# The down projection of tiles 2 to 4 as seven half-size products, with the sums on GpSimd

## The chip, the cores and the metric

The kernel runs on one core of a Trainium2 chip. The metric is the device time of one execution in microseconds (us). The engines are TensorE (PE, with its weight loads PEld), VectorE (DVE), ScalarE (ACT), GpSimd (POOL) and SyncE (SP), which here only issues transfers. A kernel of this size can be told from another by about 0.2%.

## The reference

A layer of 2048 tokens with 512 features: normalisation, 32 heads of sliding-window attention (16 features a head, window 256) with an output projection, and beside it a gated feed-forward network of 1792 hidden features whose result gates the attention's. All data are float32.

```python
xn = _layernorm(x, axis=-1)
qkv = (xn @ wqkv).reshape(B, S, 3, H, Dh).transpose(2, 0, 3, 1, 4)
scores = jnp.einsum("bhqd,bhkd->bhqk", q, k) * (Dh ** -0.5)
mask = (idx[:, None] - idx[None, :] >= 0) & (idx[:, None] - idx[None, :] < 256)
o = softmax(where(mask, scores, -1e9)) @ v
s = o @ wo
h = silu(xn @ w1) * (xn @ w3)
out = h @ w2
return x + s * silu(out)
```

## The kernel before

**Precision.** Each float32 operand is cut into two float16 halves, the value rounded (ACT casts) and the remainder (POOL or DVE subtracts). A product is then three matmuls: high x high, high x low, low x high. A cut tile is 128 x 1024 float16, high half first.

**Tiles.** The tokens go in four tiles of 512 (`NT`), counted 0 to 3 in the code. The hidden features go in 14 blocks of 128 (`FB`), in `GROUPS` whose down projections are summed in one bank each. For each tile and block, `gate_up` makes gate and up (24 matmuls of 512 columns), ACT takes a tanh (L867), DVE multiplies twice (L871, L876), ACT casts the hidden block (L880) and POOL subtracts its remainder (L300, by the helper `halves`, in two pieces of 256 columns). For each group, `down` runs over the four blocks of 128 tokens: three matmuls of 512 columns for each hidden block into one bank (L901). The first group's bank is copied by ACT (L914), the others are added by DVE (L917) to a sum in SBUF. `total` then gates: tanh of the sum (L937), a product on DVE (L938), the output projection of the attention (L943), a product with its bank (L947), the residual (POOL by `halves`, for the last tile DVE at L949), and the store. The last block of 128 tokens of all is done by `total_by_columns` in two halves of 256 columns (L965 to L976).

**Weights.** In tile 0 the weights are measured, scaled and cut (`measure`, `measure_down`; ACT at L303 and L304, POOL at L300), and the cut weights are stored to DRAM (`dW1`, `dW2`). Tiles 1 to 3 load them again (`load`).

**Attention** runs in units of four heads beside that: scores and their maxima (L588, L600), scores, mask, exponential (L662, L669, L672) and values (L690). `normalise` sends the denominators through DRAM and multiplies on POOL (`on`, by `rb`) some 8 steps later, and ACT casts the product (L740).

**Order.** PE takes its instructions in the order of the code (`ORDERED`). `feed_forward` lists the dense pieces, `spread` mixes them among the attention's batches, and a group's `down` comes after the next block's `gate_up`. For DVE, ACT, POOL and SP a scheduler sets the order beforehand; each engine then works through its own queue strictly in that order. Work for later is put off by `later(n, f)`, n steps on. All temporary tiles lie in `SLOTS` equal slots of SBUF: `take` hands out the one that was given back longest ago, and its new user waits for the last reader of the old tile. PSUM has two banks for the dense work, used in turn (`bank`).

## Time and profile before

| | before |
|---|---|
| median of 3 runs | 840.06 us (839.98 to 840.22) |
| span of the profiled execution | 835.6 us |
| start of tile 1's gate and up, about | 221 us |
| end of the last attention values | 800.8 us |
| first matmul of the last outputs (L943) | 821.5 us |
| start of the last addition | 832.6 us |

The span is the time from the first to the last instruction of the one execution that the profiler took. Matmuls are pipelined: a matmul of 512 columns is shown with 0.38 us and starts 0.216 us after the one before it.

### The profile page before, as it was taken

How to read it: one execution, taken by the hardware profiler on the slowest of the kernel's cores; microseconds unless marked ns; L12 is line 12 of the kernel's file. 1: busy time of each engine (PE TensorE's matmuls, PEld its weight loads, DVE VectorE, ACT ScalarE, POOL GpSimd, SP SyncE). 2: the span in 40 equal slices, each digit the busy share in tenths (PEclk: the TensorE clock that was granted, in tenths of full speed). 3: DMA queues.
4: the chain of work that ended last, by engine and by line, in shares of the span. 5: the costliest groups of instructions: out<-in, count | busy, mean ns of one | idle time of the engine just before them, and what ended most of it. 6: DMA issues, size and time to landing. Idle time of an engine off the chain costs nothing.

```text
span 835.6 us, 22584 instructions
## 1 busy us (share of the span) xinstructions
PE 809.6 (97%) x8750; PEld 381.5 (46%) x8750; DVE 614.4 (74%) x2034; ACT 408.2 (49%) x598; POOL 196.7 (24%) x325
## 2 busy tenths in 40 slices
PE   9999898899999999999999999999999999999998
PEld 4434344434444444444445444444444444444444
DVE  8788767966797767798778876687777777676435
ACT  6799776373436444344433444443444443443521
POOL 2236264051313203111110211121111104031211
PEclk9999999999999999999999999999999999999999
DMA  9977556146633453453442535533443443434101
GB/s 281 260 232 237 165 181 184 47 152 199 189 96 95 110 140 108 138 155 110 130 121 72 140 94 154 142 111 102 119 143 88 112 117 107 116 96 125 55 21 52
DMA packets 95323, 110.62 MB, mean 132 GB/s; under 512 B 17200, under 2 KB 60528, under 8 KB 95216
## 3 DMA queue, kind: packets, MB, share of 16 engines
q1 hardware_dynamic: 94928, 108.67, 44.9%
q8 instruction: 68, 1.11, 0.6%
q10 hardware_dynamic: 288, 0.52, 0.2%
q14 instruction: 39, 0.32, 0.1%
HBM read 76.28 MB, written 28.57 MB: 125 GB/s over the span
## 4 chain that ended last, share of the span: by engine, by line
PE 68%; DVE 9%; issue 7%; DMA 6%; ACT 5%; POOL 3%; SPq 2%; POOLq 0%; ACTq 0%; DVEq 0%
PE m L856 24%; PE m L901 13%; PE po L690 8%; PE m L534 6%; PE s L662 5%; PE m L943 4%; PE m L504 3%; POOL slot L300 3%; DVE junk L600 2%; PE s L588 2%; DMA slot<-in_B_w_dram 2%; DMA qa<-dQ 1%; DVE s L669 1%; PE po L588 1%; ACT slot L303 1%
## 5 line engine op out<-in xcount | busy, mean ns | idle before, releaser
L300 POOL TENSOR_TENSOR slot<-slot,slot 128x256 f16<-128x256 f32 (+1 forms) x228 | 148.3, 677 | 575.7 <-ACT slot L880 464.5
L856 PE MATMUL m<-XH,slot 128*128 128x512 f16 x896 | 267.3, 380 | 4.3 <-DVE slot L547 2.5
L672 ACT ACTIVATE pt<-s,es 128x1024 f32<-128x1024 f32 x152 | 167.7, 1113 | 180.5 <-DVE s L669 177.3
L856 PEld LDWEIGHTS <-slot 128*128 128x128 f16 x1344 | 124.8, 98 | 159.9 <-issue 17.7
L856 PE MATMUL m<-XL,slot 128*128 128x512 f16 x448 | 169.8, 379 | 0.0
L901 PE MATMUL m<-slot,slot 128*128 128x512 f16 x672 | 158.1, 383 | 2.2 <-DVE slot L917 1.0
L669 DVE TENSOR_TENSOR s<-s,MK 128x256 f32<-128x256 f32 (+2 forms) x280 | 118.6, 435 | 49.2 <-PE s L662 48.2
L600 DVE CUSTOM_DVE_ANT_0 junk<-s,MW 128x320 bf16<-128x320 f32 x276 | 134.3, 486 | 24.7 <-PE s L588 15.7
L901 PEld LDWEIGHTS <-slot 128*128 128x128 f16 x672 | 62.5, 98 | 82.2 <-issue 12.3
L600 DVE CUSTOM_DVE_ANT_0 junk<-po,MW 128x320 bf16<-128x320 f32 x172 | 83.7, 487 | 5.6 <-DVE al L272 0.4
L690 PE MATMUL po<-pt,V 64*32 64x320 f32 (+4 forms) x2880 | 77.7, 343 | 0.5 <-DVE pp L277 0.5
L880 ACT CAST slot<-slot 128x512 f16<-128x512 f32 x56 | 34.5, 616 | 67.4 <-DVE slot L876 67.1
L690 PEld LDWEIGHTS po<-pt,V 64*32 64x32 f32 x2880 | 51.9, 106 | 24.1 <-PE s L588 4.7
L662 PE MATMUL s<-qa,KA 50*64 50x320 f16 (+3 forms) x1472 | 58.0, 259 | 1.4 <-DVE M L600 0.6
L871 DVE SCALAR_TENSOR_TENSOR slot<-slot,m 128x512 f32<-128x512 f32 x56 | 38.3, 684 | 28.0 <-ACT slot L867 27.0
L662 PEld LDWEIGHTS <-KA 50*64 50x64 f16 x1472 | 30.2, 105 | 55.7 <-issue 36.1
L867 ACT ACTIVATE slot<-m,sgs 128x512 f32<-128x512 f32 x56 | 38.4, 685 | 27.8 <-PE m L856 27.6
L588 PE MATMUL s<-KA,qa 48*64 48x320 f16 (+2 forms) x648 | 45.3, 294 | 6.7 <-DVE M L600 4.0
L917 DVE SCALAR_TENSOR_TENSOR slot<-m,dsc,slot 128x512 f32<-128x512 f32 x48 | 35.9, 747 | 15.9 <-PE m L901 15.6
L876 DVE SCALAR_TENSOR_TENSOR slot<-m,slot 128x512 f32<-128x512 f32 x56 | 38.5, 688 | 12.3 <-PE m L856 11.4
L534 PE MATMUL m<-XH,whi 128*128 128x512 f16 x120 | 44.7, 381 | 1.4 <-DVE slot L876 0.9
L534 PE MATMUL m<-XL,whi 128*128 128x512 f16 x120 | 44.5, 379 | 0.0
(152 smaller groups left out, 870.7 us busy)
## 6 DMA issues: line engine op xcount, KB each, us to landing
slot<-dW SPq DMA_DIRECT2D x126, 256.0 KB
slot<-in_B_w_dram SPq DMA_DIRECT2D x42, 256.0 KB
dW<-slot SPq DMA_DIRECT2D x42, 256.0 KB
slot<-in_A_x_dram SPq DMA_DIRECT2D x30, 256.0 KB
KA<-dK SPq DMA_DIRECT2D x24, 288.0 KB
qa<-dQ SPq DMA_DIRECT2D x32, 192.0 KB
dQ<-slot SPq DMA_DIRECT2D x16, 256.0 KB
dK<-slot SPq DMA_DIRECT2D x16, 256.0 KB
```

What stands on the lines that cost most here:

```text
L300: op(out[:, c], a[:, c], b[:, c])
L534: nc.tensor.matmul(cell["pp"], a[:, k, c, :], b[:, c, :], start=(c, i) == parts[0][0], stop=(c, i) == parts[-1][-1])
L588: nc.tensor.matmul(s[64 * c:64 * c + 64, r, :n], qa[rows, 2 * p + a, ii * P + 64 * c:ii * P + 64 * c + 64], ka[rows, 2 * p + a, e - n:e], ...
L600: nc.vector.tensor_tensor_reduce(out=junk[:, :n], in0=s[:, r, :n], in1=mask, scale=1.0, scalar=NEG, op0=ALU.add, op1=ALU.max, accum_out=M[ ...
L662: nc.tensor.matmul(s[64 * h:64 * h + 64, r, o:o + 64 * n], ka[rows, 2 * p + a, 64 * (m + 4):64 * (m + 5)], qa[rows, 2 * p + a, 64 * (m + k ...
L669: nc.vector.tensor_add(v, v, MK[:, kind, of:of + n, :].unsqueeze(1).to_broadcast([P, 2 * len(which), n, 64]))
L672: nc.scalar.activation(pt, s, AF.Exp, scale=es)
L690: nc.tensor.matmul(cell["po"][32 * i:32 * i + 32, h, 64 * (m + k):64 * (m + k + n)], V[64 * h:64 * h + 64, (4 * t + m // 2) % VB, hd * VW: ...
L856: nc.tensor.matmul(cell[k], w[:, (a * NC + c) * P:(a * NC + c + 1) * P], b[:, c, :], start=c == 0 and i == 0, stop=c == NC - 1 and i == 2)
L867: nc.scalar.activation(sg, cell[0], AF.Tanh, scale=sg_scale[:, f:f + 1])
L876: nc.vector.scalar_tensor_tensor(sg, cell[1], 0.5 * HS / (WS * XS)**2, sg, op0=ALU.mult, op1=ALU.mult)
L901: nc.tensor.matmul(ps, hh[:, a * TW + b * P:a * TW + (b + 1) * P], w[:, c * D:(c + 1) * D], start=f == f0 and i == 0, stop=f == f1 - 1 and ...
```

## The change

The down projection of tiles 1 to 3 is a product of a token x hidden and a hidden x output matrix. Two neighbouring hidden blocks are taken as the two halves of the inner dimension, the tile's 512 tokens as two halves of 256, the 512 outputs as two halves of 256. The 2 x 2 x 2 block product, eight half-size products, is made as seven (Strassen's scheme, in Winograd's order with 15 sums). `PRODUCTS` names them: each takes one sum of token halves on the left (`lefts`, made for every pair of blocks on POOL and cast by ACT) and one sum of weight halves on the right (`sums`, made in tile 0 on POOL, cast by ACT, stored to the new DRAM tensor `dWT`). A product has, for each of two blocks of 128 tokens and each pair of hidden blocks, three matmuls of 256 columns. Its bank goes to a sum of its own (`SUMS`), copied by ACT for the first group and added by DVE for the others. After the last group `combine` makes seven additions of 128 x 512 (on POOL, for the last tile on DVE).

The right-hand slices are loaded product by product, two products ahead (`rights`, `AHEAD`); tiles 1 to 3 no longer load `dW2` whole. Three groups of 4, 6 and 4 blocks take the place of four. Outputs are multiplied, added and stored in halves of 256 columns. The outputs of tiles 1 and 2 come two units of attention later than before. There are 46 slots, and the room for them is taken from a scratch area of the compiler's (`dynamic_dma_scratch_size`).

```diff
-SLOTS = 39
+SLOTS = 46
-GROUPS = ((0, 4), (4, 8), (8, 11), (11, 14))
+GROUPS = ((0, 4), (4, 10), (10, 14))
+PRODUCTS = ("12 21", "22 -4", "11 11", "s3 t3", "s1 t1", "s2 t2", "s4 22")
+LEFT = {"11": (0, 0), "12": (1, 0), "22": (1, 1), "s1": (2, 0), "s2": (2, 1), "s3": (3, 0), "s4": (3, 1)}
+RIGHT = {"11": (0, 0), "21": (1, 0), "22": (1, 1), "t1": (2, 0), "t2": (2, 1), "t3": (3, 0), "-4": (3, 1)}
+AHEAD = 2
...
+    dWT = dram.tile([FB, P, 2 * D], F16, name="dWT")
...
     def load(t, f):
         if t:
-            WF[t, f] = a, b = [take(F16) for _ in range(2)], take(F16)
+            WF[t, f] = a, _ = [take(F16) for _ in range(2)], None
             for k in range(2):
                 nc.sync.dma_start(a[k], dW1[f, k])
-            nc.sync.dma_start(b, dW2[f])
             return
...
+            def sums(f):
+                e, o = whole.pop(f), whole.pop(f + 1)
+                a, b = take(F32), take(F32)
+                left, right = slice(0, 256), slice(256, 512)
+                nc.gpsimd.tensor_sub(a[:, left], e[:, right], e[:, left])
+                nc.gpsimd.tensor_sub(a[:, right], o[:, right], a[:, left])
+                nc.gpsimd.tensor_sub(b[:, left], o[:, right], e[:, right])
+                nc.gpsimd.tensor_sub(b[:, right], o[:, left], a[:, right])
+                give(e, o, after=5)
+                for i, raw in enumerate((a, b)):
+                    made = take(F16)
+                    nc.scalar.copy(made[:, 0:D], raw)
+                    halves(nc.gpsimd.tensor_sub, made[:, D:], raw, made[:, 0:D])
+                    nc.sync.dma_start(dWT[f + i], made)
+                    give(raw, made, after=6)
             for i, f in enumerate(range(f0, f1)):
                 later(1 + 2 * i, lambda f=f: cut(f))
+                if f % 2:
+                    later(2 * n + 2 + 4 * i, lambda f=f: sums(f - 1))
...
+    def lefts(t, f):
+        e, o = WHOLE.pop((t, f)), WHOLE.pop((t, f + 1))
+        a, b = take(F32), take(F32)
+        one, two = slice(0, 256), slice(256, 512)
+        def cast(i, raw, c):
+            made = LH[t, f][i]
+            nc.scalar.copy(made[:, c], raw[:, c])
+        def rest(i, raw, c):
+            made = LH[t, f][i]
+            nc.gpsimd.tensor_sub(made[:, D + c.start:D + c.stop], raw[:, c], made[:, c])
+        LH[t, f] = [take(F16), HH.pop((t, f + 1)), take(F16), take(F16)]
+        cast(1, o, slice(0, 512))
+        cast(0, e, one)
+        nc.gpsimd.tensor_add(a[:, one], e[:, two], o[:, two])
+        nc.gpsimd.tensor_sub(b[:, one], e[:, one], e[:, two])
+        nc.gpsimd.tensor_sub(a[:, two], a[:, one], e[:, one])
+        nc.gpsimd.tensor_sub(b[:, two], o[:, one], a[:, two])
+        cast(3, b, slice(0, 512))
+        cast(2, a, slice(0, 512))
+        for i, raw, c in ((1, o, one), (1, o, two), (0, e, one), (3, b, one), (2, a, one), (2, a, two), (3, b, two)):
+            rest(i, raw, c)
+        give(e, o, a, b, after=5)
...
-                later(1, rest)
+                if t == 0:
+                    later(1, rest)
+                elif f % 2:
+                    later(1, lambda: lefts(t, f - 1))
...
+    def rights(t, k, p):
+        i, which = RIGHT[PRODUCTS[p].split()[1]]
+        c = slice(256 * which, 256 * which + 256)
+        f0, f1 = GROUPS[k]
+        made = []
+        for j in range(f0, f1, 4):
+            slot = take(F16)
+            made.append(slot)
+            for n, f in enumerate(range(j, min(j + 4, f1), 2)):
+                src = (dW2[f], dW2[f + 1], dWT[f], dWT[f + 1])[i]
+                nc.sync.dma_start(slot[:, n * D:(n + 1) * D].rearrange("p (a c) -> p a c", a=2),
+                                  src.rearrange("p (a c) -> p a c", a=2)[:, :, c])
+        RIGHTS[t, k, p] = made
+
+    def product(t, k, p):
+        f0, f1 = GROUPS[k]
+        i, which = LEFT[PRODUCTS[p].split()[0]]
+        def part():
+            ps = bank([P, 2, 256])
+            right = RIGHTS.pop((t, k, p))
+            fs = range(f0, f1, 2)
+            for blk in range(2):
+                q = 256 * which + 128 * blk
+                for f in fs:
+                    n = (f - f0) // 2
+                    l, r = LH[t, f][i], right[n // 2][:, (n % 2) * D:(n % 2 + 1) * D]
+                    for x, (a, c) in enumerate(((0, 0), (0, 1), (1, 0))):
+                        nc.tensor.matmul(ps[:, blk, :], l[:, a * D + q:a * D + q + 128], r[:, 256 * c:256 * c + 256],
+                                         start=f == f0 and x == 0, stop=f == f1 - 2 and x == 2)
+            give(*right)
...
+            if k == 0:
+                SUMS[t, p] = take(F32)
+                with urgent():
+                    nc.scalar.activation(SUMS[t, p], flat, AF.Copy, scale=down_scale[:, 0:1])
+            else:
+                with urgent():
+                    nc.vector.scalar_tensor_tensor(SUMS[t, p], flat, down_scale[:, k:k + 1], SUMS[t, p],
+                                                   op0=ALU.mult, op1=ALU.add)
+            if (k, p) == (len(GROUPS) - 1, len(PRODUCTS) - 1):
+                combine(t)
+        return [(3 * (f1 - f0) // 2, part)]
+
+    def combine(t):
+        p2, p4, p1, p7, p5, p6, p3 = (SUMS.pop((t, p)) for p in range(7))
+        def add(a, b):
+            if t == NT - 1:
+                nc.vector.tensor_add(a, a, b)
+            else:
+                halves(nc.gpsimd.tensor_add, a, a, b)
+        add(p2, p1)
+        add(p6, p1)
+        add(p3, p5)
+        add(p3, p6)
+        add(p7, p6)
+        add(p4, p7)
+        add(p5, p7)
...
             if half:
-                with urgent():
-                    nc.vector.scalar_tensor_tensor(y, ps, sc["y"], y, op0=ALU.mult, op1=ALU.mult)
...
+                for i, c in enumerate((slice(0, 256), slice(256, 512))):
+                    with urgent():
+                        nc.vector.scalar_tensor_tensor(y[i], ps[:, c], sc["y"], y[i], op0=ALU.mult, op1=ALU.mult)
+                    (nc.vector if t == NT - 1 else nc.gpsimd).tensor_add(y[i], y[i], XR[t, b][:, c])
+                    nc.sync.dma_start(out[r, c], y[i])
...
+                for _ in range(3 if len(late) == len(PRODUCTS) else 2):
+                    if late:
+                        pieces += products(*late.pop(0))
...
-        if 2 <= n % 8 < 6 and t:
-            beside[n] += [(0, lambda t=t, b=n % 8 - 2: residual(t - 1, b))] + total(t - 1, n % 8 - 2)
+        b = n % 8 - (2 if t == 1 else 4)
+        if 0 <= b < 4 and t:
+            beside[n] += [(0, lambda t=t, b=b: residual(t - 1, b))] + total(t - 1, b)
```

In the changed kernel the lines are L681 for the exponential, L884 and L888 for the casts and remainders of `lefts`, L892 to L895 for its sums, L854 to L857 for `sums`, L1015 for the products' matmuls, L1025 and L1028 for the sums of their banks, L1041 for the combination on DVE, L1077 for the gate's product, L1107 and L1128 for the outputs.

## The prediction

> **What bounds the kernel now.** I read the cores' line first (one core, its clock), then busy time by stretch, then the groups of instructions, then the waits, and last the timeline of two places: the first use of the down weights, near 77 us, and the end. The cores' line and the page's first part:

> ```profile
> core 0: 835.6 us, clock 0.998
> PE 809.6 (97%) x8750; PEld 381.5 (46%) x8750; DVE 614.4 (74%) x2034; ACT 408.2 (49%) x598; POOL 196.7 (24%) x325
> ```

> Busy time by stretch (stretch, its length, then PE, PEld, DVE, ACT and POOL, PE clock, DMA share, GB/s):

> ```profile
> 60.00:100.00 40.00, 35.76 (x316) 16.17 (x315) 32.88 (x132) 34.58 (x67) 20.56 (x32) 0.96 0.70 228
> 100.00:200.00 100.00, 90.99 (x1044) 43.79 (x1042) 75.00 (x296) 59.40 (x99) 38.67 (x60) 1.00 0.44 134
> 300.00:400.00 100.00, 98.25 (x1158) 46.15 (x1157) 82.15 (x260) 42.70 (x53) 18.86 (x28) 1.00 0.46 129
> 500.00:600.00 100.00, 100.00 (x1111) 46.51 (x1109) 72.43 (x230) 44.20 (x54) 18.92 (x29) 1.00 0.46 130
> ```

> The granted clock is full, so an average is not hiding a throttle. From 200 us on PE never rests and no other engine passes 82%: there a shorter matmul stream shortens the kernel. Up to 200 us PE is 89 to 91% busy, and between 60 and 100 us ACT is at 86% with DVE at 82%: there PE waits for others, and work added to ACT or POOL can cost time.

> **What the change does to PE.** Each of the tiles 2 to 4 spends 14 blocks x 4 token blocks x 3 = 168 matmuls of 512 columns on the down projection, 504 together. They become 7 products x 7 pairs of blocks x 2 x 3 = 294 a tile, 882 together, of 256 columns. The before kernel already runs 256-column matmuls with fresh weights each time, in its last block (timeline, PE and its weight loads):

> ```profile
> 821.47 7.93 PE L943 MATMUL m<-slot,slot 128*128 128x512 f16 x36
> 829.03 2.72 PEld L972 LDWEIGHTS <-slot 128*128 128x128 f16 x24
> 829.24 2.78 PE L972 MATMUL m<-slot,slot 128*128 128x256 f16 x24
> L901 PE MATMUL m<-slot,slot 128*128 128x512 f16 x672 | 158.1, 383 | 2.2 <-DVE slot L917 1.0
> ```

> The durations overlap, so I take the distance: (7.93 - 0.38) / 35 = 0.2157 us for 512 columns, and, with 0.27 for one, (2.78 - 0.27) / 23 = 0.109 us for 256. The weight load in between (2.72 / 24 is one every 0.11 us) stays covered. So 504 x 0.2157 - 882 x 0.109 = 108.7 - 96.1 = **12.6 us less**. Seven products instead of eight would give 13.6; half-size matmuls give 1 us of it back. If a weight load were laid bare each time the distance would be about 0.2 and the change would lose 70 us; 24 in a row at 0.109 exclude that.

> Fewer, longer dense pieces also mean fewer changes between them and attention: in PE's order 156 places after, 167 before. A change costs about 0.09: in the rows of 77 us below, the sixth matmul of a run of six starts at 77.28 + 5 x 0.216 = 78.36, and the next one 0.31 after it, not 0.216. 11 x 0.09 = **1.0 us less**.

> **What it adds.** POOL's order has 292 element-wise instructions before and 523 after, ACT's has 65 more, and SP issues 955 transfers for 821. The prices:

> ```profile
> L300 POOL TENSOR_TENSOR slot<-slot,slot 128x256 f16<-128x256 f32 (+1 forms) x228 | 148.3, 677 | 575.7 <-ACT slot L880 464.5
> L880 ACT CAST slot<-slot 128x512 f16<-128x512 f32 x56 | 34.5, 616 | 67.4 <-DVE slot L876 67.1
> L917 DVE SCALAR_TENSOR_TENSOR slot<-m,dsc,slot 128x512 f32<-128x512 f32 x48 | 35.9, 747 | 15.9 <-PE m L901 15.6
> ```

> POOL grows by 231 x 0.68 = 157 us, to 354 us or 43%; ACT by about 65 x 0.62 = 40, to 54%. Neither becomes the bound by its total. What counts is who waits in their queues.

> *The first tile.* Its matmuls are unchanged, but the weight sums (`sums`) go into POOL's queue among the cuts that PE needs. POOL before, where the down weights of the first four blocks are cut (slots 36, 37, 38 and 9 hold blocks 0 to 3; the other rows are other tiles):

> ```order
> L300 TENSOR_TENSOR slot20_1153<-slot36_732,slot20_1153 128x256 x2
> L300 TENSOR_TENSOR slot0_1165<-slot35_729,slot0_1165 128x256 x2
> L300 TENSOR_TENSOR slot21_1186<-slot37_734,slot21_1186 128x256 x2
> L300 TENSOR_TENSOR slot27_1243<-slot38_736,slot27_1243 128x256 x2
> L300 TENSOR_TENSOR slot26_1256<-slot30_1182,slot26_1256 128x256 x2
> L300 TENSOR_TENSOR slot23_1269<-slot9_824,slot23_1269 128x256 x2
> ```

> and POOL after, from just behind the cut of block 0 (blocks 1, 2, 3 are slots 37, 38, 1; one more sum stands ahead of it):

> ```order
> L855 TENSOR_TENSOR slot7_1421<-slot37_735,slot7_1421 128x256
> L856 TENSOR_TENSOR slot31_1422<-slot37_735,slot36_733 128x256
> L857 TENSOR_TENSOR slot31_1422<-slot37_735,slot7_1421 128x256
> L309 TENSOR_TENSOR slot28_1187<-slot37_735,slot28_1187 128x256 x2
> L309 TENSOR_TENSOR slot18_1244<-slot38_737,slot18_1244 128x256 x2
> L309 TENSOR_TENSOR slot19_1257<-slot15_1183,slot19_1257 128x256 x2
> L854 TENSOR_TENSOR slot15_1585<-slot38_737 128x256
> L856 TENSOR_TENSOR slot9_1586<-slot1_825,slot38_737 128x256
> L855 TENSOR_TENSOR slot15_1585<-slot1_825,slot15_1585 128x256
> L857 TENSOR_TENSOR slot9_1586<-slot1_825,slot15_1585 128x256
> L309 TENSOR_TENSOR slot20_1270<-slot1_825,slot20_1270 128x256 x2
> ```

> Eight sums now stand ahead of the cut of block 3. The timeline there, PE and POOL of before:

> ```profile
> 77.28 1.46 PE L901 MATMUL m<-slot,slot 128*128 128x512 f16 x6
> 78.67 0.42 PE L662 MATMUL s<-qa,KA 50*64 50x320 f16 x10
> 79.30 5.51 PE L901 MATMUL m<-slot,slot 128*128 128x512 f16 x24
> 91.71 0.25 PE L588 MATMUL s<-KA,qa 48*64 48x128 f16 x4 [2.92 <-DVE M L600]
> 74.31 3.82 POOL L300 TENSOR_TENSOR slot<-slot,slot 128x256 f16<-128x256 f32 x6 [0.44 <-ACT slot L304]
> 78.67 1.30 POOL L300 TENSOR_TENSOR slot<-slot,slot 128x256 f16<-128x256 f32 x2 [0.54 <-ACT slot L304]
> ```

> The cut of block 3 ends at 78.67 + 1.30 = 79.97 and PE comes to it at 79.30 + 3 x 0.216 = 79.95: nothing to spare, and POOL nearly without a pause before. Eight sums at 0.64 (six in 3.82) are 5.1 us, less the half microsecond POOL stood idle: PE stands about 4.5 us. At 91.71 it waited 2.92 us for DVE's maxima, and DVE can work its backlog off in the new hole, so some returns. Bounds 0 and 4.5; I take **+2.5**.

> *The chain for each pair of blocks, tiles 2 to 4.* `lefts` adds on POOL what ACT casts next. ACT before, at a comparable place (L672 is the exponential, L880 the cast):

> ```order
> L700 COPY os_4986<-po_4937 128x512
> L880 CAST slot6_5004<-slot11_4907 128x512
> L672 ACTIVATE pt_5025<-s_5015,es1_409 128x1024
> L867 ACTIVATE slot35_5049<-m0_5036,sgs_153 128x512
> L937 ACTIVATE slot19_5258<-slot1_1418 128x512
> L672 ACTIVATE pt_5070<-s_5059,es1_409 128x1024
> ```

> and after (L681 is the exponential, L884 the casts, of which the second and third read POOL's sums):

> ```order
> L924 ACTIVATE slot31_5501<-m1_5409,sgs_154 128x512
> L1067 ACTIVATE slot39_5742<-slot33_1455 128x512
> L681 ACTIVATE pt_5515<-s_5505,es1_410 128x1024
> L884 CAST slot34_5545<-slot31_5501 128x512
> L884 CAST slot19_5553<-slot8_5550 128x512
> L884 CAST slot1_5554<-slot42_5551 128x512
> L681 ACTIVATE pt_5588<-s_5577,es1_410 128x1024
> ```

> Two casts that wait for POOL now stand ahead of an exponential. POOL needs two additions for the first and two instructions more for the second, 1.4 and 2.7 us, against 0.62 for the cast in between: ACT stands some 1.4 us a pair, 21 pairs, 30 us. The waits of before price such a stand:

> ```profile
> ACT pt L672 <- DVE s L669: 177.3, 111, 5.3
> ACT slot L740 <- POOL on L300: 24.8, 11, 4.3
> PE s L588 <- ACT pt L672: 1.9, 3, 0.7
> POOL on L300 <- DMA rb<-de: 33.4, 6, 11.6
> ```

> (who waits, total us, times, longest). ACT already stood 24.8 us for POOL, and PE's wait for the exponential came to 1.9: ACT usually stands idle until DVE hands it the scores. By that share 30 us cost 2.3; the bounds are 0 and 5, the last if the casts themselves hurt as well. I take **+2.0**.

> *Banks and transfers.* A four-block product fills its bank in 12 x 0.109 = 1.31 us, so the bank after next must be empty by then. At the end a bank's last column passes at 826.65 (24 matmuls of L943), and DVE is through with it at 827.61:

> ```profile
> 826.86 0.75 DVE L947 SCALAR_TENSOR_TENSOR slot<-m,us,slot 128x512 f32<-128x512 f32 x1 [1.11 <-PE m L943]
> ```

> 0.96 us, so a queue of over 0.35 on DVE costs PE time. Only some 18 places in PE's order have no attention in between. With the right-hand slices, now fetched two products ahead, **+1.0**, between 0 and 3.

> *The end.* The last gate and up block is followed by seven products with no attention, then by the outputs. Before:

> ```profile
> 813.07 8.56 PE L901 MATMUL m<-slot,slot 128*128 128x512 f16 x36
> 813.27 0.69 DVE L876 SCALAR_TENSOR_TENSOR slot<-m,slot 128x512 f32<-128x512 f32 x1 [1.18 <-PE m L856]
> 823.66 0.69 DVE L966 SCALAR_TENSOR_TENSOR slot<-slot,slot 128x512 f32<-128x512 f32 x1 [0.69 <-ACT slot L965]
> 824.27 0.75 DVE L947 SCALAR_TENSOR_TENSOR slot<-m,us,slot 128x512 f32<-128x512 f32 x1
> 825.05 0.69 DVE L949 TENSOR_TENSOR slot<-slot,slot 128x512 f32<-128x512 f32 x1
> 830.84 0.48 DVE L974 SCALAR_TENSOR_TENSOR slot<-m,us,slot 128x256 f32<-128x256 f32 x1
> 831.35 0.42 DVE L975 TENSOR_TENSOR slot<-slot,slot 128x256 f32<-128x256 f32 x1
> 832.58 0.42 DVE L975 TENSOR_TENSOR slot<-slot,slot 128x256 f32<-128x256 f32 x1
> ```

> The 36 matmuls take 821.47 - 813.07 = 8.40 us, 0.63 over their 7.77: the wait for the last cast. After, the first product needs the last pair's sums: 0.89 until DVE is done, then three instructions of POOL (2.1) and hand-overs, 3.1 us, while PE has five matmuls (0.55) to do: it stands 2.5, that is 1.9 more. Then DVE, with L1028 the banks' sums, L1041 the combination, L1107 the outputs:

> ```order
> L1028 SCALAR_TENSOR_TENSOR slot0_12302<-m1_13573,dsc_156,slot0_12302 128x512
> L1041 TENSOR_TENSOR slot17_12066<-slot17_12066,slot8_12219 128x512
> L1041 TENSOR_TENSOR slot0_12302<-slot0_12302,slot43_12125 128x512
> L1041 TENSOR_TENSOR slot4_11830<-slot4_11830,slot17_12066 128x512
> L1041 TENSOR_TENSOR slot0_12302<-slot0_12302,slot8_12219 128x512
> L1107 SCALAR_TENSOR_TENSOR slot10_13601<-m0_13600,us_4361,slot10_13601 128x256
> ```

> where before the last sum (L917) one gate product and then the outputs came:

> ```order
> L917 SCALAR_TENSOR_TENSOR slot29_11383<-m0_12604,dsc_155,slot29_11383 128x512
> L966 SCALAR_TENSOR_TENSOR slot8_12680<-slot8_12680,slot29_11383 128x512
> L947 SCALAR_TENSOR_TENSOR slot15_12622<-m1_12621,us_4227,slot15_12622 128x512
> L949 TENSOR_TENSOR slot15_12622<-slot15_12622,slot28_12485 128x512
> L947 SCALAR_TENSOR_TENSOR slot32_12643<-m0_12642,us_4227,slot32_12643 128x512
> ```

> From the last product's end DVE has 25 instructions: that sum, 5 of the combination, 3 gate products, 8 outputs and 8 additions of 256 columns. Independent neighbours follow at 0.61 (823.66 to 824.27), dependent ones at 0.78 and 0.51 (824.27 to 825.05, 830.84 to 831.35). With independent spacing (0.41 and 0.35 for the short ones, their durations less the same 0.07) that is 0.4 + 9 x 0.61 + 8 x 0.41 + 8 x 0.35 = 12 us, with a few dependences 12.5; with dependent spacing throughout 14.6. Then as before 2.6 from the last addition's start (833.0) to the end. So 15.1 to 17.2, against 835.6 - 821.47 = 14.1. Most neighbours are independent: +1.4. The end costs **+3.3**, between 2.9 and 5.

> **The sum.** 835.6 - 12.6 - 1.0 + 2.5 + 2.0 + 1.0 + 3.3 = 830.8 for the profiled execution. The median of the runs (840.06) lies 4.4 above that span, which the change does not touch: **835.2 us**.

> **Rivals.** *GpSimd as the gate (slower).* POOL's queue now holds, one behind the other, the normalising products that wait for a chain of transfers (six waits, 33.4 us, up to 11.6) and the sums that ACT and PE need. While POOL stands for `rb`, ACT stands at the next cast and the exponential behind it is late. Before, nothing urgent stood behind such a wait. If four of the six come back at 5.6 us each and half of each reaches PE (11 us), I get 846. It decides from 4.9 us of stalls beyond those charged. For it: ACT at 86% and POOL without pause near 77 us. Against it: the scheduler places those products late, and 10 of 16 did not wait.

> [...]

> [...]

> [...]

> *Everything hides (faster).* First tile, exponentials and banks cost nothing and the end its lower bound: -12.6 - 1.0 + 2.9, 829.4. *The terms cancel.* Stalls near their upper bounds: no change.

> That fewer columns are not streamed is excluded by the order itself.

> **How the numbers follow.** Under 0.2% (1.7 us) a measurement of this kernel does not tell from none, so the borders are 838.4 and 841.7. Forecast 0.43 (its own range 830 to 838), everything hides 0.10, cancel 0.12, GpSimd as the gate 0.30, ports 0.05. Faster 0.53, same 0.12, slower 0.35. The range of 8 in 10 reaches from just under the fast rival to a little over the gate's 846: 829 to 848.

> **What would show it.** Products at 0.109 us and PE at 98% from 200 us on: the main term. A stand of PE near 80 us at block 3's cut: the first tile. Waits of PE for the exponential of no more than 5 us: the chain. More than 15 us from the last product to the end: the end's term. I am wrong if PE shows new idle time between 200 and 800 us released by ACT or POOL, or if the time from the start of tile 2 to the last attention does not shrink by about 10 us.

## The result: 886 us, slower by 46

The changed kernel takes 885.97 us (median of 4 runs, 884.5 to 886.86) against 840.02 for the kernel before on the same chip: a ratio of 1.056, with an interval of 1.054 to 1.057. The forecast was 835.2, its range ended at 848.

The profiled execution spans 885.1 us where it was 835.6. The cores' line and the page's first part, of the changed kernel:

```profile
core 0: 885.1 us, clock 0.974
PE 819.5 (93%) x9124; PEld 426.0 (48%) x9124; DVE 627.1 (71%) x2050; ACT 438.2 (50%) x663; POOL 352.4 (40%) x556
```

GpSimd's total came out as forecast (354), and no engine is full over the whole span. But TensorE fell from 97 to 93% busy, and its mean granted clock from 0.998 to 0.974. By stretch (columns as in the prediction):

```profile
60.00:100.00 40.00, 33.70 (x294) 14.77 (x283) 34.38 (x121) 33.67 (x64) 31.59 (x48) 0.91 0.69 225
100.00:200.00 100.00, 82.62 (x902) 38.98 (x901) 68.08 (x257) 57.96 (x100) 50.01 (x76) 0.95 0.46 145
300.00:400.00 100.00, 93.68 (x1091) 47.51 (x1090) 71.89 (x233) 48.76 (x65) 38.02 (x58) 0.98 0.45 124
500.00:600.00 100.00, 98.18 (x1144) 51.60 (x1141) 72.12 (x229) 49.33 (x66) 43.12 (x65) 1.00 0.43 115
```

Only the third tile (500 to 600 us) looks as foreseen. The products and the waits that the prediction named, from the groups and from the waits of the changed kernel (who waits, for whom, total us, times, longest):

```profile
L1015 PE MATMUL m<-slot,slot 128*128 128x256 f16 x882 | 108.4, 278 | 6.3 <-ACT slot L884 4.7
```

```profile
PE s L597 <- ACT pt L681: 14.7, 12, 4.0
PE s L671 <- ACT pt L681: 6.9, 5, 2.4
ACT slot L884 <- POOL slot L894: 27.0, 21, 4.6
ACT slot L884 <- POOL slot L895: 9.2, 14, 0.7
POOL on L309 <- DMA rb<-de: 59.5, 10, 13.3
DVE dr L736 <- DMA dr<-dd: 18.2, 9, 4.2
```

TensorE waits 21.6 us for exponentials (2.4 before), ScalarE 36 us for GpSimd's sums (30 forecast). The median distance between two products' matmuls is 0.109 us, as forecast; all their distances together make 113.6 us, not 96.1.

**Where the time goes**, by the distances from each matmul's start to the next (sums over a run's trace, us):

| matmuls | before | grouping alone | no sums | changed |
|---|---|---|---|---|
| gate and up | 304.9 | 314.8 | 316.5 | 318.0 |
| down, products included | 155.6 | 152.8 | 148.7 | 162.0 |
| scores (two lines) | 96.6 | 97.6 | 102.5 | 119.1 |
| all the rest | 274.7 | 272.7 | 277.3 | 281.9 |
| start of the last matmul | 831.8 | 837.8 | 844.9 | 881.0 |

("Grouping alone" is the run x1 and "no sums" the run z3, both told below.) A stand is time in which an engine waits. The changed kernel's time went to almost every line, most of all to the scores.

**Three places of the changed kernel**, read across engines. First, the use of block 3's cut; PE, ACT and POOL in turn:

```profile
82.08 1.04 PE L963 MATMUL m<-slot,slot 128*128 128x512 f16 x4
84.66 1.67 PE L963 MATMUL m<-slot,slot 128*128 128x512 f16 x7 [1.55 <-POOL slot L309]
80.23 1.14 ACT L861 CAST slot<-slot 128x512 f16<-128x512 f32 x2
83.39 0.62 ACT L861 CAST slot<-slot 128x512 f16<-128x512 f32 x1 [2.02 <-POOL slot L857]
81.81 0.72 POOL L855 TENSOR_TENSOR slot<-slot,slot 128x256 f32<-128x256 f32 x1
82.61 0.74 POOL L857 TENSOR_TENSOR slot<-slot,slot 128x256 f32<-128x256 f32 x1
83.32 13.34 POOL L309 TENSOR_TENSOR slot<-slot,slot 128x256 f16<-128x256 f32 x20
```

GpSimd makes the sums (L855, L857) while TensorE comes to the cut behind them and stands 1.55 us. That was forecast. Not forecast is the last row: 13 us of cuts and remainders queue up behind them without a pause. Second, the start of the fourth tile, POOL, ACT and PE:

```profile
728.17 8.26 POOL L309 TENSOR_TENSOR slot<-slot,slot 128x256 f32<-128x256 f32 x12
738.44 0.72 POOL L894 TENSOR_TENSOR slot<-slot,slot 128x256 f32<-128x256 f32 x1
739.19 0.62 ACT L884 CAST slot<-slot 128x512 f16<-128x512 f32 x1 [4.56 <-POOL slot L894]
741.02 1.11 ACT L681 ACTIVATE pt<-s,es 128x1024 f32<-128x1024 f32 x1
742.18 0.48 PE L597 MATMUL s<-KA,qa 48*64 48x320 f16 x4 [3.96 <-ACT pt L681]
```

The combination of the third tile (12 of its 14 halves, 8.26 us) delays the sums of a pair, the cast stands 4.56 us for them, the exponential behind the cast is late, TensorE stands 3.96. Third, the end, DVE and then PE:

```profile
855.87 0.35 DVE L736 RECIPROCAL dr<-dr 128x32 f32<-128x32 f32 x1 [4.20 <-DMA dr<-dd]
856.40 0.68 DVE L933 SCALAR_TENSOR_TENSOR slot<-m,slot 128x512 f32<-128x512 f32 x1
857.79 0.61 PE L1015 MATMUL m<-slot,slot 128*128 128x256 f16 x2 [4.65 <-ACT slot L884]
859.37 10.89 PE L1015 MATMUL m<-slot,slot 128*128 128x256 f16 x79 [0.97 <-POOL slot L888]
```

VectorE stood 4.20 us for a transfer of the normalisation, with the last gate product (L933) queued behind it; so the last pair's operands came late. SyncE's queue shows how that transfer (L732) was issued:

```profile
850.28 0.52 SPq L719 DMA_DIRECT2D dd<-os  x1
850.90 1.24 SPq L996 DMA_DIRECT2D slot<-dWT  x2
852.24 1.21 SPq L996 DMA_DIRECT2D slot<-dW  x2
853.55 0.54 SPq L732 DMA_DIRECT2D dr<-dd  x1
```

Between the store of the denominators and their load stand four loads of half rows for the products (L996), 2.45 us of issuing. In the run x3 below the store goes out at 829.50 and the load at 831.22, and the reciprocal does not wait.

### The profile page after: what moved, and what is told of

Its sections match the earlier page's. It is cut to its first block, busy times and chain, and to the rows that moved or that the text cites. A ratio compares the mean times of both kernels' runs of the same rounds, so it can differ in the third digit from the quotient of the medians.

```text
span 885.1 us, 23936 instructions
## 1 busy us (share of the span) xinstructions
PE 819.5 (93%) x9124; PEld 426.0 (48%) x9124; DVE 627.1 (71%) x2050; ACT 438.2 (50%) x663; POOL 352.4 (40%) x556
## 4 chain that ended last, share of the span: by engine, by line
PE 49%; POOL 12%; DVE 10%; ACT 9%; DMA 8%; issue 8%; SPq 3%; ACTq 0%; POOLq 0%; DVEq 0%
PE m L913 20%; POOL slot L309 7%; PE po L699 6%; PE m L1015 6%; PE m L543 5%; ACT pt L681 3%; PE s L671 3%; PE m L1102 2%; DVE junk L609 2%; PE m L513 2%; DMA dr<-dd 2%; DVE s L678 2%; PE s L597 2%; SPq L996 1%; ACT slot L312 1%
## 5 line engine op out<-in xcount | busy, mean ns | idle before, releaser
L913 PE MATMUL m<-XH,slot 128*128 128x512 f16 x896 | 271.1, 385 | 9.4 <-DVE slot L556 2.6
L681 ACT ACTIVATE pt<-s,es 128x1024 f32<-128x1024 f32 x152 | 167.6, 1112 | 161.4 <-DVE s L678 160.3
L913 PEld LDWEIGHTS <-slot 128*128 128x128 f16 x1344 | 125.3, 98 | 166.1 <-issue 27.3
L309 POOL TENSOR_TENSOR slot<-slot,slot 128x256 f16<-128x256 f32 (+1 forms) x176 | 114.9, 687 | 139.4 <-ACT slot L939 45.4
L1015 PE MATMUL m<-slot,slot 128*128 128x256 f16 x882 | 108.4, 278 | 6.3 <-ACT slot L884 4.7
L1015 PEld LDWEIGHTS <-slot 128*128 128x128 f16 x882 | 86.2, 100 | 27.9 <-ACT slot L884 4.9
L884 ACT CAST slot<-slot 128x256 f16<-128x256 f32 (+1 forms) x84 | 47.4, 564 | 98.5 <-DVE slot L933 61.9
L888 POOL TENSOR_TENSOR slot<-slot,slot 128x256 f16<-128x256 f32 x147 | 95.5, 673 | 1.6 <-ACT slot L884 1.5
L892 POOL TENSOR_TENSOR slot<-slot,slot 128x256 f32<-128x256 f32 x21 | 15.3, 727 | 135.0 <-DVE slot L933 135.0
L928 DVE SCALAR_TENSOR_TENSOR slot<-slot,m 128x512 f32<-128x512 f32 x56 | 38.3, 684 | 42.4 <-ACT slot L924 40.3
L893 POOL TENSOR_TENSOR slot<-slot 128x256 f32<-128x256 f32 x21 | 15.2, 725 | 131.0 <-DVE slot L933 77.5
L671 PE MATMUL s<-qa,KA 50*64 50x320 f16 (+3 forms) x1472 | 59.0, 261 | 7.4 <-ACT pt L681 6.9
L597 PE MATMUL s<-KA,qa 48*64 48x320 f16 (+2 forms) x648 | 47.4, 299 | 18.9 <-ACT pt L681 14.7
L671 PEld LDWEIGHTS <-KA 50*64 50x64 f16 x1472 | 30.9, 106 | 58.0 <-issue 43.7
L597 PEld LDWEIGHTS <-qa 48*64 48x64 f16 x1024 | 31.6, 108 | 46.2 <-issue 31.4
L924 ACT ACTIVATE slot<-m,sgs 128x512 f32<-128x512 f32 x56 | 38.3, 684 | 28.1 <-PE m L913 27.9
```

Source lines behind the costliest of these rows:

```text
L309: op(out[:, c], a[:, c], b[:, c])
L597: nc.tensor.matmul(s[64 * c:64 * c + 64, r, :n], qa[rows, 2 * p + a, ii * P + 64 * c:ii * P + 64 * c + 64], ka[rows, 2 * p + a, e - n:e], ...
L671: nc.tensor.matmul(s[64 * h:64 * h + 64, r, o:o + 64 * n], ka[rows, 2 * p + a, 64 * (m + 4):64 * (m + 5)], qa[rows, 2 * p + a, 64 * (m + k ...
L681: nc.scalar.activation(pt, s, AF.Exp, scale=es)
L884: nc.scalar.copy(made[:, c], raw[:, c])
L888: nc.gpsimd.tensor_sub(made[:, D + c.start:D + c.stop], raw[:, c], made[:, c])
```

## Experiments

Each run stands beside runs of the kernel before on its own chip; the last columns compare with those. "All" is the changed kernel. Where two runs' intervals overlap, the difference between them is not clear of noise.

| run | us | before | ratio, interval | difference |
|---|---|---|---|---|
| all | 886.0 | 840.0 | 1.056 [1.054, 1.057] | +45.9 |
| x1 grouping alone | 843.5 | 839.8 | 1.005 [1.003, 1.007] | +3.8 |
| x2 all, no weight sums | 871.6 | 839.8 | 1.040 [1.035, 1.044] | +31.8 |
| x3 all, no left sums | 863.7 | 839.8 | 1.028 [1.026, 1.030] | +24.0 |
| x4 all, last tile plain | 871.4 | 839.8 | 1.037 [1.035, 1.040] | +31.6 |
| z3 all, no sums | 851.9 | 839.0 | 1.016 [1.013, 1.019] | +12.9 |
| y1 combination on VectorE | 881.8 | 838.2 | 1.051 [1.049, 1.054] | +43.6 |
| y2 left casts later | 885.5 | 838.2 | 1.055 [1.052, 1.058] | +47.2 |
| y3 weight casts later | 878.2 | 838.2 | 1.049 [1.044, 1.054] | +40.0 |
| y4 y1 to y3 together | 877.0 | 838.2 | 1.047 [1.044, 1.050] | +38.8 |
| u1 left casts on GpSimd | 891.1 | 840.5 | 1.059 [1.054, 1.063] | +50.6 |
| u2 weight casts on GpSimd | 893.8 | 840.5 | 1.064 [1.061, 1.067] | +53.4 |
| z1 products spread | 886.0 | 839.0 | 1.056 [1.053, 1.059] | +47.0 |
| w1 normalisation later | 889.5 | 839.0 | 1.061 [1.058, 1.065] | +50.4 |
| z2 matmuls at the end | 885.5 | 839.0 | 1.056 [1.052, 1.060] | +46.5 |
| v1 no sums, no reload | 847.0 | 837.7 | 1.010 [1.008, 1.012] | +9.3 |
| v2 no sums, no combination | 848.5 | 837.7 | 1.013 [1.010, 1.016] | +10.8 |
| v3 no sums, no normalising | 851.3 | 837.7 | 1.016 [1.014, 1.017] | +13.6 |
| v4 before, no normalising | 850.3 | 837.7 | 1.012 [1.009, 1.016] | +12.6 |

How late four of the 152 exponentials start, and the end, against the profiled execution before (there at 241, 336, 682, 786 and 835.6 us):

| run | 241 | 336 | 682 | 786 | end |
|---|---|---|---|---|---|
| x1 | +4.6 | +5.3 | +6.4 | +6.3 | +6.1 |
| all | +20.1 | +29.8 | +34.2 | +41.8 | +49.4 |
| x2 | +3.1 | +12.5 | +18.5 | +26.0 | +33.4 |
| x3 | +18.4 | +24.4 | +23.6 | +25.1 | +26.9 |
| x4 | +21.7 | +24.5 | +35.4 | +35.7 | +34.8 |
| z3 | +5.1 | +11.6 | +11.2 | +11.8 | +13.3 |
| v1 | +2.0 | +7.4 | +5.3 | +5.6 | +7.3 |
| v4 | +11.9 | +14.3 | +13.5 | +13.2 | +13.5 |

The profiled span before, 835.6 us, lies 4.4 under the median of its runs, and the others mostly 1 to 3 under theirs; so the last column differs from the differences above by up to 3.5 us.

### What the parts cost

x1, in the kernel before (with it, as in the changed kernel, the downs in pieces of two blocks and the smaller scratch area):

```
-SLOTS = 39
+SLOTS = 46
-GROUPS = ((0, 4), (4, 8), (8, 11), (11, 14))
+GROUPS = ((0, 4), (4, 10), (10, 14))
```

> The kernel before with only the change's grouping of the down projection (groups of 4, 6 and 4 blocks, accumulated in pieces of two), its 46 slots and its smaller scratch for descriptors; all four tiles by ordinary products, no sums. Theory A (the weight sums by GpSimd in the first tile make that tile late, and the granted clock falls behind each stall): 836 to 842 us, the exponentials of the first tile within 3 us of the kernel before, no more than three stretches at half clock. Theory B (the six-block group alone, cut and multiplied in the first tile, makes it late): 860 us or more, with the stalls near 124 to 190 us and most of the half-clock stretches.

+3.8 us, between the theories' numbers, and most of it there by 241 us. The grouping, with the slots and the scratch area that x1 does not tell from it, has a price of its own in the first tile, but not the big one.

x2:

```
                 split_pool(b[:, 0:D], b[:, D:], raw, sw[:, f - f0:f - f0 + 1])
-                whole[f] = raw
+                give(raw, after=5)
+                nc.sync.dma_start(dWT[f], b)
```

> The changed kernel without the sums of the down weights: the cut weights themselves are written to the scratch that held the sums, so four of the seven products take wrong right-hand operands of the same size; 28 GpSimd sums, 14 casts and 28 remainder halves fall away in the first tile. Theory A: 20 to 30 us come back, 855 to 866 us, and the exponential that stood 26 us late at 300 us stands within 5 us of the kernel before. Theory B: 880 us or more. Theory E (each stall's cost is doubled by the clock) goes with A and says that the half-clock stretches ahead of 300 us, eight in the changed kernel, fall to two or less.

14.1 us come back (45.9 less 31.8), all in the first tile: at 241 us the kernel is 3.1 late, not 20.1. TensorE's row from 60 to 100 us is nearly that of the kernel before:

```profile
60.00:100.00 40.00, 34.91 (x321) 15.95 (x318) 31.54 (x123) 34.08 (x67) 20.77 (x32) 1.00 0.77 240
```

A is right about the place, though its size was put at 20 to 30. B falls. The half-clock stretches ahead of 300 us go from seven to three (mean granted clock 0.984 over the span, 0.974 in the changed kernel), where E said two at most.

x3:

```
-        a, b = take(F32), take(F32)
...
+        LH[t, f] = [he, ho, he, ho]
+        for made, raw in ((ho, o), (he, e)):
+            nc.scalar.copy(made[:, 0:TW], raw)
+            halves(nc.gpsimd.tensor_sub, made[:, TW:], raw, made[:, 0:TW])
```

> The changed kernel without the sums of the hidden rows: each pair of blocks is cut as the kernel before cuts it, and the four left-hand operands of the products are the two cut blocks twice; per pair four GpSimd sums, one cast and a remainder and a half fall away, for 21 pairs. Theory D (the chain of sums on GpSimd and ScalarE makes tiles two to four lose what the products save): 8 to 12 us come back in the tiles and 2 to 4 at the end, 869 to 876 us. Theory A alone: 880 to 885 us, the end 2 to 4 us shorter at most and the tiles unchanged.

22.0 us come back, more than either theory said, spread over all tiles: 5 by 336 us, 11 by 682, 17 by 786, and another 6 at the end (1.7 where it was 7.6, from the exponential at 786 us to the end). TensorE's waits for exponentials fall from 21.6 to 10.5:

```profile
PE s L597 <- ACT pt L681: 6.2, 7, 2.6
PE s L671 <- ACT pt L681: 4.3, 4, 2.3
```

Two things make 22.0 no pure price of the sums. At the end x3's reciprocal does not stand for its transfer, as shown above, and the sums are not what it stood for. And x3 has a stand that the changed kernel does not have, for the next tile's input (TensorE 3.14 us at 356 us; the same in z3 below).

x4:

```
-                        late = [(-1, t, k)] if t else [q for b in range(4) for q in down(t, k, b)]
+                        late = [(-1, t, k)] if 0 < t < NT - 1 else [q for b in range(4) for q in down(t, k, b)]
```

> The changed kernel with the fourth tile's down projection by ordinary products, so that only tiles two and three use the seven half-size ones. The products of the last tile cost 4.2 us more (a third of 12.6). If the end of the changed kernel (last pair's sums, the combination) costs 7 to 11 us over the kernel before, as the shift of the last exponentials against the end says: 878 to 882 us. If its stalls would only move elsewhere in the last tile: 886 to 890 us.

14.3 us come back although 4.2 us of saved matmuls (by the forecast) are given up, more than either number expected, and the kernel is no later at the end than at 786 us. The last tile was the worst place for the scheme.

z3, both edits of x2 and x3:

> The changed kernel without either kind of sums: the cut weights themselves stand for their sums, and each pair of blocks is cut as the kernel before cuts it, so that most products have wrong operands of the right size. What is left of the change is the grouping, the seven products with their reloaded operands, the combination and the outputs in halves. If the costs add: 886 less 14.4 less 22.2, 849 us, so that the products gain nothing even where the sums cost nothing, and 5 to 6 us are lost against the grouping alone (843.6). If the sums' costs overlap (each alone leaves the other's stands in place): 836 to 843 us, the products' 12.6 us appear once the sums are gone. If a third cost stands behind them both: 855 us or more.

The costs nearly add: 33.0 us come back, where 14.1 and 22.0 make 36.1. The sums are the larger part of the loss. What is left of the change, with the sums left out, is still 12.9 us slower than before and 9.1 slower than its grouping alone; some 5 us of this come with the stand at 341 us told below, which the changed kernel does not have.

### Order or amount of work

y1, y2 and y3 move sums and casts; y4 is the three together.

```
 def add(a, b):
-    if t == NT - 1:
-        nc.vector.tensor_add(a, a, b)
-    else:
-        halves(nc.gpsimd.tensor_add, a, a, b)
+    nc.vector.tensor_add(a, a, b)
```

> The changed kernel with the seven sums that combine the products of tiles two and three made by VectorE (whole rows) and not by GpSimd (halves); nothing else moves. Theory F (GpSimd's work stands in a row ahead of a cast, the cast stands on ScalarE ahead of an exponential, and TensorE waits for that): the 4.2 us stand at 738 us and the 6.8 us at half clock behind it go, and part of the stands near 500 to 530 us: 877 to 882 us. Rival G (GpSimd's and VectorE's amount of work, not its order, sets the time; VectorE gets 14 sums more): 884 to 889 us.

```
+        def second():
             cast(3, b, slice(0, 512))
             cast(2, a, slice(0, 512))
...
+        later(2, second)
```

> The changed kernel with the hidden rows' sums in two stages: the casts of the two summed operands and their remainders are issued two steps after the sums (but for the very last pair), so that ScalarE does not stand before a cast while GpSimd still makes the sum; the same instructions otherwise. Theory F: ScalarE's 27.0 and 9.2 us of waits for GpSimd's sums fall to under 10 together and TensorE's 14.7 and 6.9 us of waits for the exponential to under 10 together, with the half-clock stretches behind 290 us: 868 to 876 us. Rival G (the amount of work): 883 to 889 us. Rival H (the operands then come too late for the products): the products' row waits for ScalarE or GpSimd at more than 10 us, 886 us or more.

```
+                def second():
                     for i, raw in enumerate((a, b)):
                         made = take(F16)
                         nc.scalar.copy(made[:, 0:D], raw)
...
+                later(4, second)
```

> The changed kernel with the weight sums in two stages: the casts and remainders of a pair are issued four steps after its sums, so that ScalarE does not stand before a cast with the next weights' scaling behind it; the same instructions otherwise. Theory F: 6 to 12 us of the 14.4 that the weight sums cost come back, 874 to 880 us. Rival G (GpSimd is full from 70 to 90 us and from 150 to 180 us, and the cuts of weights wait for it whatever ScalarE does): 883 us or more, with the stands near 76, 83 and 170 us as before.

> The three edits together: combination on VectorE, casts of both kinds of sums issued later. Theory F with its parts adding up: 855 to 866 us. Rival G: 880 us or more. Faster than the kernel before it can be only if what is left of the end (7.7 us) and of the grouping (3.8 us) were less than the products' saving: not expected.

y1 gives 2.3 us: the half-clock stretch at 741 us is gone (mean granted clock 0.980 where it was 0.974), as F says, but the gain is less than F's. y3 gives 5.9 us, near F's lower end: its exponential at 241 us is 12.1 late, not 20.1. Both are hardly clear of noise: their intervals reach that of "all", and one of y3's four runs took 886.2 us. y2 gives nothing, and its waits say why it is no test of F: the cast still stands for the sum.

```profile
ACT slot L884 <- POOL slot L894: 26.6, 21, 4.1
```

Only TensorE keeps the order in which the kernel is written; on the other engines the scheduler sets the order, and a cast issued later can land where it was. y4 gives 7.1 us, about what the three give together (2.3, 5.9 and -1.3) and clear of noise. It lies between F's 866 and G's 880. So the casts were taken off ScalarE altogether.

u1 (u2 does the same to the casts in `sums`):

```
-            nc.scalar.copy(made[:, c], raw[:, c])
+            if i < 2:
+                nc.scalar.copy(made[:, c], raw[:, c])
+            else:
+                for h in (one, two):
+                    nc.gpsimd.tensor_copy(made[:, h], raw[:, h])
```

> The changed kernel with the casts of the two summed left-hand operands of each pair made by GpSimd, in halves, and not by ScalarE: 42 casts leave ScalarE, 84 come to GpSimd (no row shows a cast there; by its other 128x256 rows, 0.67 to 0.73 us, 56 to 61 us more of it). Theory F (what costs is that ScalarE stands for GpSimd's sums with an exponential behind; GpSimd itself has room): ScalarE's waits of 27.0 and 9.2 us for the sums go, TensorE's 14.7 and 6.9 us for the exponential fall to under 10 together, 870 to 879 us. Rival G (GpSimd's amount of work sets when operands come): 888 us or more, TensorE waits at the products for GpSimd.

> The changed kernel with the casts of the weight sums made by GpSimd, in halves, and not by ScalarE: 14 casts leave ScalarE, 28 come to GpSimd (some 20 us more of it, where it is full from 70 to 90 us and from 150 to 180 us). Theory F (ScalarE standing for GpSimd with the next weights' scaling behind): 5 to 9 us less, 877 to 881 us. Rival G (GpSimd's amount of work in the first tile): 889 us or more, the exponential at 241 us another 3 us or more later than in the changed kernel.

Both get slower, by 4.7 and 7.4 us against "all"; only u2's is clear of noise. In u1 ScalarE no longer waits for a sum of the hidden rows, yet TensorE still waits for the exponential, and GpSimd has 32 us more to do (its group of casts, and PE's waits):

```profile
L888 POOL CAST slot<-slot 128x256 f16<-128x256 f32 x84 | 32.2, 398 | 1.3
```

```profile
PE s L597 <- ACT pt L681: 9.0, 8, 2.6
PE s L671 <- ACT pt L681: 9.0, 5, 3.3
```

In u2 it is 28 casts, some 11 us at that mean, and the first tile is where they land; 70 to 90 us, first of the changed kernel, then of u2:

```profile
70.00:90.00 20.00, 16.45 (x125) 6.92 (x131) 17.29 (x62) 16.92 (x30) 19.84 (x32) 0.91 0.54 182
```

```profile
70.00:90.00 20.00, 10.21 (x79) 4.29 (x77) 16.87 (x53) 13.35 (x24) 19.70 (x34) 0.87 0.40 127
```

GpSimd is full in both (19.84 and 19.70 of 20 us), and in u2 TensorE works 10.2 us and not 16.4. The loss stands there at once: TensorE waits 6.85 us for block 3's cut, 1.55 in the changed kernel. Ahead of that cut GpSimd now has casts (some 2 us) and four remainder halves more than before (2.5 us). So in the first tile GpSimd's queue at that place is a gate, as rival G says, by what is in it and by its order (y3 too). For tiles two to four u1 shows less. VectorE's waits for the reciprocal's transfer (`dr`) rise from 18.2 to 31.8 us in it, and TensorE stands 2.44 us at 297 us and 6.02 at 861 just behind two of them; so u1 does not tell what 32 us more of GpSimd cost from what these later transfers cost.

### The rest

z1 and w1, in the changed kernel:

```
-                pieces += gate_up(t, f)
...
+                    pieces += both[:2] + products(*late.pop(0)) + both[2:] + products(*late.pop(0))
```

> The changed kernel with the products of a group spread: from the second block behind a group on, one product stands between the gate and the up half of a block and one behind it, not two in a row; the same instructions. Theory P (short products in a row finish faster than VectorE and ScalarE empty their banks, 1.3 us of matmuls to 0.75 us of eviction beside the attention's own work, and the piece behind stands for a bank): the stands of about 1 us behind products (315, 487, 562, 723 us and others, some 8 us in all) go: 876 to 881 us. Rival (they are the first three products behind a group, which stay in a row, or the evictions are late whatever the order): 883 to 888 us.

The time does not change. But the stands did not go, as P wanted; they moved. Behind products TensorE loses 6.1 us at eight places where gate and up follow, 4.7 at seven in the changed kernel, and now waits for gate and up's own bank (DVE L928, 5.8 us where it was 1.7). So P's price is not tested.

```
-            halves(nc.gpsimd.tensor_mul, on, on, rb)
+            later(8, lambda: halves(nc.gpsimd.tensor_mul, on, on, rb))
...
-        later(8, invert)
+        later(14, invert)
```

> The changed kernel with the attention's normalisation issued later: the reciprocal 14 steps and not 8 after the unit, GpSimd's multiplication by the broadcast reciprocals another 8 steps on, the cut at 28 and not 24; the same instructions. Theory N (steps are counted in pieces, a half-size product is a shorter piece, so VectorE and GpSimd now come to the normalisation before its transfers have landed, and the sums and evictions behind it wait): VectorE's 18.2 us and GpSimd's 59.5 us of waits for these two transfers fall to under 6 and under 25, TensorE's stands behind 290 us shrink, and the last pair's operands, now held up by the reciprocal for 4.2 us at 855 us, are ready earlier: 868 to 877 us. Rival G (the amount of work on GpSimd and VectorE sets the time, waits only move): 882 to 887 us.

Slower than the changed kernel by 4.4 us, with the waits that it was to remove still there (`dr` again 18.2 us, `rb` 68.0 where it was 59.5): like y2 it did not do what it was made for, so it does not test N.

v1, v2, v3 start from z3, v4 from the kernel before. v1 loads each group's rows whole, once; v2 leaves the seven additions out; v3 and v4 replace the normalisation:

```
-            for n, f in enumerate(range(j, min(j + 4, f1), 2)):
-                src = (dW2[f], dW2[f + 1], dWT[f], dWT[f + 1])[i]
...
+            for f in range(f0, f1):
+                RIGHTS[t, f] = slot = take(F16)
+                nc.sync.dma_start(slot, dW2[f])
```

> The changed kernel without sums (as in the run without either kind, 851.9 us), and with the right-hand operands loaded once for a group as whole rows (14 loads of 256 KB a tile, as the kernel before has them, in place of 21 pairs of half rows for each product); the products take quarters of these. Theory T (the half-row reloads, 12 MB more and 38 thousand packets more on one queue, make the other transfers land late, for which VectorE and GpSimd then stand): 840 to 846 us, VectorE's waits for transfers (13.4 and 10.2 us in the run without sums) fall to about the kernel before's 3.4 and 3.3. Rival (the transfers are covered): 850 to 854 us.

```
-        add(p2, p1)
...
-        add(p5, p7)
```

> The changed kernel without sums and also without the seven additions that combine a tile's products (four of the seven accumulators go to the output as they are). Theory C (the combination, 14 halves of GpSimd's in a row at the start of the tile behind, 7 rows of VectorE's at the end, holds up evictions and the end): 4 to 7 us under the 851.9 us of the run without sums, 845 to 848 us, more than half of it at the end. Rival: 850 to 853 us, the end shorter by less than 2 us.

```
         def invert():
-            nc.vector.reciprocal(dr, dr)
...
+            halves(nc.gpsimd.tensor_mul, on, on, on)
```

> The changed kernel without sums and with the attention's normalisation cut off from its transfers: no reciprocal, no round trip of the sums of the exponentials through memory; GpSimd multiplies the rows by themselves instead. Theory N (half-size products change when the normalisation's transfers are waited for, so that VectorE and GpSimd stand for them with evictions behind): 6 to 10 us under 851.9 us, 842 to 846 us, and the same edit in the kernel before gains 2 us at most. Rival: both fall by the same, 0 to 3 us.

> The kernel before with the same edit: normalisation cut off from its transfers. The control for the run above. Theory N: 838 to 840 us, since VectorE stands only 3.4 us for these transfers there. Rival: it gains as much as the run above.

v1 gives 3.6 us and v2 2.1 against z3 (v2's interval overlaps z3's), v3 none. v1's time misses T's range, and VectorE's waits for transfers stay at 10.6 and 8.6 us, where T wanted about 3. v4 is the surprise: the kernel before, with work taken *away*, is 12.6 us slower, and the second table shows that almost all of this is there by 241 us and nothing is added behind 336 us. A likely reading, not followed through, is that leaving instructions out moves the others: in every run without weight sums the exponential at 241 us is 2 to 12 us later than before. So the 2 to 4 us of v1, v2 and y1 can't be taken as prices of one part, x2's 14.1 is uncertain by several us for the same reason, and N stays open.

One stand that x1 does not have can be read in z3, around its exponential at 344 us; DVE, SP and PE:

```profile
340.62 0.69 DVE L415 BATCH_NORM_STATS2 st<-slot 128x6 f32<-128x512 f32 x1 [5.01 <-DMA slot<-in_A_x_dram]
342.49 0.67 DVE L893 SCALAR_TENSOR_TENSOR slot<-slot,m 128x512 f32<-128x512 f32 x1
332.20 2.40 SPq L1074 DMA_DIRECT2D out_dram<-slot  x2
335.24 0.42 SPq L411 DMA_DIRECT2D slot<-in_A_x_dram  x1
343.21 0.38 PE L543 MATMUL m<-XH,whi 128*128 128x512 f16 x1 [3.61 <-DVE slot L893]
```

The next tile's input is issued at 335.24, behind the outputs' halves on the same queue; VectorE has come to it and stands 5.01 us with a gate product (L893) behind it, and TensorE stands 3.61. The same jump, of 5 to 7 us between 310 and 336 us, is in v1, v2 and x3 too, all of them without the left sums; the changed kernel has none of that size there.

### The clock

z2:

```
         pieces += [(0, lambda p=p: rights(t, k, p)) for p in range(AHEAD)]
+        pieces.append((0, lambda: keep_busy(20)))
```

> The changed kernel with 20 matmuls of ones (4.3 us at full clock, their result unused) ahead of the last group's first product, where TensorE stands 4.9 us for the last pair's operands. Theory E (the granted clock halves behind a stand of TensorE and doubles the price of what follows): the 6.8 us at half clock from 856.9 us go or shrink to 3.4, 2 to 3.5 us come back, 881 to 883 us. Rival (the clock has another cause, or TensorE's work there is not what the end waits for): 884 to 887 us with the half-clock stretch in place.

Two stretches at the end, of the changed kernel and then of z2:

```profile
850.00:856.80 6.80, 3.14 (x17) 1.37 (x14) 1.59 (x4) 0.69 (x1) 0.00 (x0) 1.00 0.52 146
857.00:863.70 6.70, 4.94 (x23) 3.22 (x24) 0.89 (x3) 1.85 (x3) 5.90 (x10) 0.50 0.26 54
```

```profile
850.00:857.00 7.00, 7.00 (x35) 3.15 (x33) 1.54 (x4) 0.69 (x1) 0.00 (x0) 1.00 0.50 139
857.00:863.70 6.70, 5.60 (x48) 4.31 (x47) 2.31 (x4) 1.86 (x3) 5.91 (x9) 1.00 0.29 69
```

Kept busy, TensorE has its full clock behind the stand and makes 48 matmuls where it made 23; all products together take 109.5 us and not 113.6. E is right about the clock, and its rival about the time. The time does not move: VectorE, at the outputs' gate behind ScalarE, holds up a bank, and the last products stand for it:

```profile
869.31 1.47 PE L1015 MATMUL m<-slot,slot 128*128 128x256 f16 x12 [2.18 <-DVE slot L1028]
```

The end is VectorE's, so a faster TensorE gains nothing there (885.5 us for 886.0).

No version here that makes the whole layer beats the kernel before; the nearest is x1, without the scheme.

## Why the prediction was wrong

**The saving (12.6 us): the distance right, the size off.** The distance is 0.109 and the weight loads stay covered (882 of them, 100 ns each on average). In z3, without sums, the products of the three tiles take 106.8 us. The downs of the same tiles take 113.7 before and 111.6 in x1. So the saving is 6.9 us, or 4.8 against the same grouping. The forecast compared ideal streams, 108.7 with 96.1. The downs run 4.9 us over that before (2.9 in x1), the products 10.6 in z3. Of this 2.1 us are 22 changes to the scores (L671), the same in all three. New are 4.9 us at seven places where gate and up follow a product, mostly because a bank is not yet empty (0.35 before), and 2.7 us within the products, most of it for the last pair. Two of these places in z3, where L556 empties a projection's bank and L990 a product's:

```profile
468.70 0.59 PE L878 MATMUL m<-XH,slot 128*128 128x512 f16 x2 [1.04 <-DVE slot L556]
542.82 0.59 PE L878 MATMUL m<-XH,slot 128*128 128x512 f16 x2 [1.01 <-ACT slot L990]
```

**First tile (+2.5, bounds 0 to 4.5): the step that failed first.** Removing the weight sums gives 14.1. The prediction priced one place, block 3's cut. There it was fair: TensorE stood 1.55 us. But the first tile has three groups of such sums, with remainders, in a queue that already ran without a pause. Each group adds to it: against x2 the changed kernel is 5.8 us later at 102 us, 12.4 at 173 and 14.4 at 217. The upper bound covered one stand, not the queue. u2 shows the queue as such: with some 4.5 us more in it ahead of the same cut, TensorE stands 6.85 us there.

**The chain for each pair (+2.0, bounds 0 to 5): the step that failed most.** Removing the left sums gives 22.0 (with x3's cautions), of which 6 belong to the end. The count was right, 36 us of ScalarE's stands for 30. What failed was "by that share 30 us cost 2.3": the share came from stands that met an idle ScalarE, and TensorE's wait for exponentials came to 21.6. The term also counted only ScalarE's stands. u1, which removes them and gives GpSimd 32 us more, gains nothing; by how much of that GpSimd's own work has a price that the term lacked stays open.

**Banks and transfers (+1.0, 0 to 3): too small.** At the seven places behind products TensorE loses 4.7 us in the changed kernel. The prediction had only the products' own banks in view; two of the three longest waits are for a projection's. Loading the rows once gave 3.6 us in a kernel without sums, which the caution at v4 bounds. What the half-row loads cost besides is not settled, but at the end four of them stood ahead of the normalisation's load.

**The end (+3.3, to 5): 7.6**, from the exponential at 786 us to the end. VectorE's part was about right: from the last product's end (870.27) to the end 14.8 us, forecast 15.1 to 17.2. TensorE's stands for the last pair were 4.65 and 0.97, not 2.5, because the reciprocal and its transfer stood ahead of the gate product on VectorE; the prediction named a wait for the normalisation's transfers only for GpSimd. Behind them the clock was at half for 6.8 us.

**Not charged at all:** the grouping, 3.8; and the clock. In the changed kernel ten stretches of 3.4 or 6.8 us inside the span, 44 us together, run at half clock (one of 3.4 before). The dense matmuls in them take some 14 us beyond their median distances, against 1.6 before: one of 512 columns starts 0.427 us after the one before it, not 0.216. This is part of the prices above, not a further one: each stand was priced at its own length, and paid for again behind it.

**The chance of 0.05 for "ports"**, that more work on GpSimd lengthens VectorE's: this was not shown. With GpSimd busy for 352.4 us and not 196.7, VectorE's two rows of short maxima instructions (128x16; L605 and L606 before, L614 and L615 after) take 16.0 us together for 16.5 before. One other of VectorE's rows (L424 before, L433 after) grew from 560 to 698 ns, 2.2 us in all; its cause was not followed.

**The rival "GpSimd as the gate"** had the direction and much of the mechanism (ScalarE's casts stood behind GpSimd's queue, and the exponentials behind them), with 11 us for sums that cost 33. Its waits for `rb` did rise, 33.4 to 59.5 us, but they are 63.0 in z3, which is 34 us faster: these waits alone do not make the loss. Under its own criteria, waits for exponentials of more than 5 us, new idle time between 200 and 800 us, and no shrinking behind tile 2, the prediction was wrong at each.

The parts do not close. z3 is 9.1 us over x1 although its products take 4.8 us less than x1's downs, so some 14 us are left that v1 to v3 only touch. TensorE's stand of 3.61 us that ends at 343 us, with the half clock behind it (from 343.86 us on L543's matmuls start 0.41 and 0.42 us apart, not 0.21 to 0.22), is one that is seen; how much of the others is the order being upset, as in v4, stays open.
